# Strassen's seven products for a second group of tokens, and weight sums taken from the fp16 weights, in a fused attention and feed-forward kernel

## The chip, the cores and the metric

The kernel runs on one core of a Trainium2 chip. The metric is the device time of one execution in microseconds (us). The five engines of the core each have a queue of their own and take their instructions in order: TensorE (PE, matrix products; PEld is its weight load), VectorE (DVE), ScalarE (ACT), GpSimd (POOL) and SyncE (SP, which here only issues DMAs). An instruction that has to wait holds up all that stands behind it on its engine.

## The reference, cut to what matters

```python
for b in range(nb):                       # blocks of 64 positions
    intra = einsum('bhic,bhjc->bhij', qb, kb) * Dmask
    intra = einsum('bhij,bhjd->bhid', intra, vb)
    inter = einsum('bhid,bhde->bhie', qb * lam_pow, kv_state)
    out[:, :, sl] = intra + inter
    kv_state = lam_block * kv_state + einsum('bhsd,bhse->bhde', kb * rev_pow, vb)
...
h = x @ w_in                              # x: 3072 x 512 tokens, w_in: 512 x 2048
g = 0.5 * h * (1.0 + tanh(c * (h + 0.044715 * h * h * h)))
return g @ w_out                          # w_out: 2048 x 512
```

A decayed linear attention (4 batches, 8 heads, 768 positions, 64 columns a head) is followed by a feed-forward layer. The change concerns the last product, `g @ w_out`, for some of the tokens.

## The kernel before, in words

**Attention.** The work is cut into 24 steps (4 batches, 3 blocks of 256 positions, 2 halves of the heads). For step s, `prep` (L202) makes the decayed fp16 operands: q on DVE (L225), k on ACT (L230), v on POOL (L215). Steps 0 to 8 transpose them on PE (`stage_t`, L246, copied out at L253 or L255), later ones with a DMA (L234). `R(n, s)` (L590) issues the scores of step n (L275), the products of n and s (L310, L324, L333), the copy of the step's output to `xT` (L352, ACT) and the causal mask (L284, DVE, `PT`), then the update of the running state: `t` on DVE (L369, L372) and `u` on POOL (L379). `U(n)` does the second update. There is one buffer for the scores `Sps`, and there are six banks of PSUM for all else.

**Feed-forward.** Seven groups of tokens, of 512, 256, 256, 512, 512, 512 and 512. `queue_group(g)` appends small pieces of a group's work to a list, `filler`, and `fill(n)` pops n of them between the parts of attention, so that PE has work while other engines make its operands. The order is thus written out by hand: what `fill` issues, on every engine, stands in the engines' queues at that place. A piece `mm1` (L403) makes two of sixteen rows of blocks of the hidden layer for a group of 256 tokens (8 matmuls, L407) and their gelu (ACT, L411) into `gT`.

The second product is done in one of two ways. `mm2` (L416) is the plain one: for a tile of 128 tokens, 16 matmuls 512 wide (L422), 4 to a piece, then a copy (ACT, L428) and a DMA out (L429). `product` (L458) is Strassen's scheme: `gT` and `w_out` are cut in 2 x 2 blocks and seven products are made, each a piece of 8 matmuls 256 wide (L476). They need sums of blocks of `gT` (`sum_g`, L452, DVE, fp16, five sums, in two batches of hidden rows where the group has 256 tokens) and of `w_out` (`sum_wout`, L119). Products 3 and 4 take plain `gT` and a sum of weights, 5 and 2 a sum of `gT` (`gs`) and plain weights, 1, 7 and 6 sums on both sides. After product 2, ACT copies bank B (`m`, L483, L484) and DVE makes two sums with bank A (L487, L488); after product 1 DVE adds bank C (L496), after 6 bank D (L508), and the output leaves (L511). `behind(k, ...)` (L560) puts a batch of `sum_g` behind piece k of the group, counted from 0: for 256 tokens behind piece 5 (hidden rows 0 to 3) and piece 8 (rows 4 to 7); piece 8 is the first product, 3.

Before the change, groups 0 and 1 take `mm2`, groups 2 to 6 `product`.

**Weights.** `w_out` arrives by DMA in four parts of fp32 (`wo`, order 0, 2, 1, 3) and is cast to fp16, `w_out16`, by POOL and ACT (L115, L117). `sum_wout(j, m, eng)` makes half of one of the five sums of weight blocks on DVE (L123) from the fp32 parts: half 0 from parts 0 and 2, half 1 from parts 1 and 3. The five sums of half 0 stand ahead of step 4 (L666), those of half 1 in steps 8, 9 and 10 (L710).

The lines around the change are L662 to L713. Step n below is the turn of the loop at L699 with that n (steps 4 to 7 are written out above it). Sums are named (half, product): (1, 4) is the sum for product 4, half 1.

Of the kernel before, what the change touches and what calls it, by code (L numbers as in the profile page):

```python
# [15 lines left out]
def kernel(  # L16
# [11 lines left out]
    pin = tc.keep_in_program_order  # L28
# [32 lines left out]
    def load_step(s):  # L61
# [3 lines left out]
        for nm, src in (("q", q), ("k", k), ("v", v)):  # L65
# [8 lines left out]
    w_out16 = w16p.tile([P, NF, DM], FP16)  # L74


    HF, HE = NF // 2, DM // 2
    w_sum16 = w16p.tile([P, 5, HF, HE], FP16)
    W_SUMS = {3: ((0, 1), ALU.subtract, (1, 1)), 4: ((1, 0), ALU.subtract, (0, 0)),
              1: ((0, 0), ALU.add, (1, 1)), 7: ((1, 0), ALU.add, (1, 1)),  # L80
              6: ((0, 0), ALU.add, (0, 1))}
    w_slot = {m: i for i, m in enumerate(W_SUMS)}
    wstage = {}
# [25 lines left out]
    def cast_wout(j, eng):  # L109
        t = wstage[("o", j)]  # L110
        for i in range(2):
            dst = w_out16[:, 4 * j + 2 * i : 4 * j + 2 * i + 2, :]
            src = t[:, 2 * i : 2 * i + 2, :]
            if eng[i] is nc.scalar:
                pin(nc.scalar.activation(out=dst, in_=src, func=AF.Copy))  # L115
            else:
                pin(nc.gpsimd.tensor_copy(out=dst, in_=src))  # L117

    def sum_wout(j, m, eng):  # L119

        (f0, e0), op, (f1, e1) = W_SUMS[m]
        a, b = wstage[("o", j + 2 * f0)], wstage[("o", j + 2 * f1)]
        pin(eng.tensor_tensor(w_sum16[:, w_slot[m], 4 * j : 4 * j + 4, :],  # L123
                              a[:, :, e0 * HE : e0 * HE + HE], b[:, :, e1 * HE : e1 * HE + HE], op))


    lam_in = const.tile([P, H], FP32)
# [74 lines left out]
    def prep(s):  # L202
        prep_qk(s)
        prep_v(s)
# [8 lines left out]
    def prep_v(s):  # L213
        tv = a16p.tile([P, 2, HH, D], FP16, tag="v16", name=f"v16_{s}")
        pin(nc.gpsimd.tensor_tensor(wide(tv[:]), ld32[s][2][:], decay(dv, s), ALU.mult))  # L215
        a16[s] = a16[s] + (tv,)
        if s >= 6:
            load_ahead(s + 3)

    def prep_qk(s):  # L220
        q32, k32, _ = ld32[s]
        tqk = a16p.tile([P, 2, 2, HH, D], FP16, tag="qk16", name=f"qk16_{s}")
        tq, tk = tqk[:, 0], tqk[:, 1]
        q_eng = nc.gpsimd if s == 3 else nc.vector
        pin(q_eng.tensor_tensor(wide(tq), q32[:], decay(dq, s), ALU.mult))  # L225
        if s == 0:
            inverse(halves[0])
            odd(halves[1])
            inverse(halves[1])
        pin(nc.scalar.activation(out=wide(tk), in_=k32[:], func=AF.Copy))  # L230
        a16[s] = (tq, tk)
        if s >= FIRST_DMA_T:
            o = qkp.tile([P, 2, 2, 2, P], FP16, tag="qkT", name=f"qkT_{s}")
            pin(nc.sync.dma_start_transpose(out=o[:].rearrange("p a j h t -> p (a j h) t"),  # L234
                                            in_=tqk[:].rearrange("p a j h d -> p (a j h d)")))
            qkT[s] = o

    def stage_t(s):
        if s >= FIRST_DMA_T:
            return  # L240
        tq, tk = a16[s][:2]
        Tps = ps_M.tile([P, 2, 2, 2, P], FP16, tag="M", name="Tps")
        for i, t in enumerate((tq, tk)):
            for hp in range(2):
                for j in range(2):
                    pin(nc.tensor.transpose(Tps[:, i, j, hp, :], t[:, j, 2 * hp : 2 * hp + 2, :],  # L246
                                            ident[:]))
        o = qkp.tile([P, 2, 2, 2, P], FP16, tag="qkT", name=f"qkT_{s}")
        if s in (2, 3):
            pin(nc.scalar.activation(out=o[:, 0], in_=Tps[:, 0], func=AF.Copy))  # L250
            pin(nc.vector.tensor_copy(out=o[:, 1], in_=Tps[:, 1]))
        elif s in (1, 5, 6):
            pin(nc.scalar.activation(out=o[:], in_=Tps[:], func=AF.Copy))  # L253
        else:
            pin(nc.vector.tensor_copy(out=o[:], in_=Tps[:]))  # L255
        qkT[s] = o
# [131 lines left out]
    filler = []  # L388

    def queue_group(g):  # L390
        N = len(groups[g]) * SB
        NTAU = N // P
# [10 lines left out]
        def mm1(fs):  # L403
            Hps = ps_M.tile([P, per, N], FP32, tag="M", name="Hps")
            for i, f in enumerate(fs):
                for c in range(NC):
                    pin(nc.tensor.matmul(by_block(Hps[:, i, :]), w_in16[:, c, f * P : (f + 1) * P],  # L407
                                         x(c), start=(c == 0), stop=(c == NC - 1)))
            f = fs[0]
            dst = gT[:, f, :, :] if per == 2 else gT[:, f % HF, f // HF : f // HF + 1, :]  # L410
            pin(nc.scalar.activation(out=dst, in_=Hps[:], func=AF.Gelu_apprx_tanh))  # L411
# [4 lines left out]
        def mm2(tau, part):  # L416

            if not O2.get(tau):
                O2[tau] = [ps_M.tile([P, DM], FP32, tag="M", name="O2ps"), 0]
            for f in range(4 * part, 4 * part + 4):  # L420
                n = O2[tau][1]
                pin(nc.tensor.matmul(O2[tau][0][:], gT[:, f % HF, f // HF, tau * P : (tau + 1) * P],  # L422
                                     w_out16[:, f, :], start=(n == 0), stop=(n == NF - 1)))
                O2[tau][1] += 1
            if O2[tau][1] < NF:
                return
            o32 = otp.tile([P, DM], FP32, tag="o32", name="o32")
            pin(nc.scalar.activation(out=o32[:], in_=O2.pop(tau)[0][:], func=AF.Copy))  # L428
            pin(nc.sync.dma_start(out=out[row0 + tau * P : row0 + tau * P + P, :], in_=o32[:]))  # L429
# [115 lines left out]
        for i in range(HF):  # L545
            for fs in ([[i, i + HF]] if per == 2 else [[i], [i + HF]]):
                filler.append(lambda fs=fs: mm1(fs))
        if g == 1:
            for tau in range(NTAU):
                for part in (0, 2, 1, 3):  # L550
                    filler.append(lambda tau=tau, part=part: mm2(tau, part))
            return
        ms = ((3, 4, 5, 2), (1, 7, 6))
        order = [(m, p) for p in range(HN // P) for m in ms[0] + ms[1]]
        if g == len(groups) - 1:
# [30 lines left out]
    def fill(n):  # L586
        for _ in range(min(n, len(filler))):
            filler.pop(0)()

    def R(n, s):  # L590
        if n is not None:
            scores(n)
        products(n, s)
        if n is not None:
            causal(n)
        if s is not None and s % 2 == 1:
            g, i = group_of[s // 2]
            if i == len(groups[g]) - 1 and g > 0:
                queue_group(g)
        if n is not None:  # L600
            update(n, 0)

    def U(n):
        update(n, 1)
# [40 lines left out]
    update(3, 0)  # L645
    causal(3)
    queue_group(0)
    fill(8)
    cast_win(0, 0, 256, 256, c23, on_act=True)
# [13 lines left out]
        cast_win(j)  # L663
    DVE, ACT, POOL = nc.vector, nc.scalar, nc.gpsimd
    cast_wout(0, (POOL, POOL))
    for m in W_SUMS:  # L666
        sum_wout(0, m, DVE)
    fill(8)
    cast_wout(2, (ACT, ACT))
    cast_wout(1, (POOL, ACT))  # L670
    cast_wout(3, (POOL, ACT))
    fill(9)
    prep(4)
    stage_t(4)
    prep(5)
    fill(2)
    R(4, None)
    stage_t(5)
# [4 lines left out]
    stage_t(6)  # L683
    U(5)
    prep(7)
    fill(2)
    R(6, 5)
    U(6)
# [1 line left out]
    prep(8)  # L690
    fill(1)
    stage_t(7)
    fill(2)
    R(7, 6)
    U(7)
# [3 lines left out]
    for n in range(8, NSTEP + 1):  # L699
        m = n if n < NSTEP else None  # L700
        if m is not None:
            stage_t(n)
        if n + 2 < NSTEP:
            prep(n + 2)
        fill(2 if n <= 12 else 4)
        R(m, n - 1)
        fill(1)
        if m is not None:
            U(m)
        for p in {8: (3, 4), 9: (1, 7), 10: (6,)}.get(n, ()):  # L710
            sum_wout(1, p, DVE)
        fill(2 if n == 11 or n > 12 and n % 2 else 3)
    fill(len(filler))  # L713

# [28 lines left out]
```

## Time and profile before

| what | value |
|---|---|
| median of 6 executions | 205.3 us (204.9 to 205.92) |
| the profiled execution, its own time | 205.3 us |
| its span in the profile | 203.5 us |
| PE / DVE / ACT / POOL busy | 195.6 / 144.8 / 108.2 / 69.9 us |
| share of PE in the chain that ended last | 89% |
| L422, matmul 512 wide | 96 instructions, 21.9 us |
| L123, sum of weights | 10 instructions, 6 in 7.9 us and 4 in 6.0 us |
| L452, sum of `gT`, 128x512 | 50 instructions, 21.6 us |

The span runs from the first to the last instruction on the core; the execution's own time has 1.8 us more around it. Times in views are counted from the start of the span. In a timeline a row gives start, duration, engine, line, operation, output and inputs, shapes, count, and in brackets how long the engine had been idle and what ended that. Rows of one kind that follow each other are merged, so a row of "x2" has the time from the first's start to the last's end. A row's duration includes time in which the instruction has been issued and cannot go on. In the chain of waits a row gives start, length, engine, tile, line and number of instructions.

### The profile page before, as it was taken

The numbers are of one execution on the slowest core, as the hardware profiler recorded it, in microseconds if no ns is written. First come the engines' busy times: TensorE is split into PE (matmuls) and PEld (weight loads), VectorE is DVE, ScalarE is ACT, GpSimd is POOL, SyncE is SP. The second block draws the span as 40 slices with busy tenths as digits, with TensorE's granted clock in tenths as the row PEclk, the third lists the DMA queues.
The fourth block names the chain that finished last, engine by engine and source line by source line (L and its number), as shares of the span: only waits on it lengthen the run. The fifth ranks groups of instructions, "written<-read, shape, count | busy, mean of one in ns | idle before, by whom it ended". The sixth has DMA issues, their size and how long they took to land.

```text
span 203.5 us, 5595 instructions
## 1 busy us (share of the span) xinstructions
PE 195.6 (96%) x2325; PEld 127.6 (63%) x2325; DVE 144.8 (71%) x275; ACT 108.2 (53%) x204; POOL 69.9 (34%) x80
## 2 busy tenths in 40 slices
PE   7788999999999999999999999999999999999993
PEld 2456544456875788644688654788554788545882
DVE  4896726877699998929997828996739773236652
ACT  3365778475873573477722387641576431666210
POOL 4595123656586851336134404314412101000000
PEclk9999999999999999999999999999999999999999
DMA  5999999999999999997659993648340003300014
GB/s 151 297 324 389 385 386 377 284 291 311 333 257 231 291 247 147 233 277 184 64 155 228 236 264 95 147 114 134 87 97 0 3 0 103 108 0 0 3 47 159
DMA packets 63937, 37.85 MB, mean 186 GB/s; under 512 B 17576, under 2 KB 59048, under 8 KB 63912
## 3 DMA queue, kind: packets, MB, share of 16 engines
q1 hardware_dynamic: 63616, 37.23, 71.7%
q8 instruction: 18, 0.29, 0.6%
q10 hardware_dynamic: 296, 0.26, 0.4%
q14 instruction: 7, 0.06, 0.1%
HBM read 27.26 MB, written 6.29 MB: 165 GB/s over the span
## 4 chain that ended last, share of the span: by engine, by line
PE 89%; SPq 4%; DMA 4%; issue 1%; DVE 1%; ACT 1%
PE Hps L407 37%; PE O2ps L422 10%; PE MB L476 8%; PE MA L476 7%; PE MD L476 7%; SPq L68 4%; PE MC L476 4%; DMA wi<-in_moe_w_in_dram 4%; PE Sps L275 3%; PE Hps L522 3%; PE OK L333 3%; PE OK L324 3%; PE Tps L246 1%; PE OK L310 1%; PE ME L476 0%
## 5 line engine op out<-in xcount | busy, mean ns | idle before, releaser
L407 PE MATMUL Hps<-xT,w_in 128*128 128x512 f16 (+1 forms) x416 | 79.1, 346 | 0.0
L411 ACT ACTIVATE gT<-Hps 128x512 f16<-128x512 f32 x88 | 52.4, 597 | 22.6 <-PE Hps L407 21.8
L407 PEld LDWEIGHTS <-w_in 128*128 128x128 f16 x416 | 40.3, 98 | 33.5
L379 POOL TENSOR_TENSOR u<-t,lumask 128x256 f16<-128x256 f32 x40 | 31.3, 788 | 80.0 <-DVE t L372 53.4
L452 DVE TENSOR_TENSOR gs<-gT 128x512 f16<-128x512 f16 (+1 forms) x70 | 36.6, 587 | 10.8 <-ACT gT L411 10.6
L284 DVE TENSOR_TENSOR PT<-Sps,mask 128x1024 f16<-128x1024 f32 x24 | 29.2, 1217 | 16.9 <-PE Sps L275 16.8
L476 PEld LDWEIGHTS <-gs 128*128 128x128 f16 x360 | 34.9, 98 | 4.0
L215 POOL TENSOR_TENSOR v<-v,dv 128x512 f16<-128x512 f32 x24 | 29.2, 1218 | 4.2 <-DMA v<-in_v_dram 3.8
L352 ACT ACTIVATE xT<-OK 128x256 f16<-128x256 f32 x47 | 18.1, 453 | 18.9 <-PE OK L333 15.3
L422 PE MATMUL O2ps<-w_out,gT 128*128 128x512 f16 x96 | 21.9, 379 | 0.0
L230 ACT ACTIVATE qk<-k 128x512 f16<-128x512 f32 x24 | 15.0, 624 | 8.0 <-DMA k<-in_k_dram 8.0
L225 DVE TENSOR_TENSOR qk<-q,dq 128x512 f16<-128x512 f32 x23 | 19.2, 835 | 0.0
L483 ACT ACTIVATE m<-MB 128x512 f32<-128x512 f32 x9 | 5.4, 597 | 25.4 <-PE MB L476 25.4
L476 PE MATMUL MA<-w_sum,gT 128*128 128x256 f16 x144 | 17.5, 273 | 0.1
L476 PE MATMUL MD<-w_sum,gs 128*128 128x256 f16 x136 | 17.5, 273 | 0.0
L476 PE MATMUL MB<-w_out,gs 128*128 128x256 f16 x144 | 17.2, 273 | 0.0
L476 PEld LDWEIGHTS <-gT 128*128 128x128 f16 x144 | 14.0, 98 | 2.8 <-ACT gT L411 0.3
L422 PEld LDWEIGHTS <-gT 128*128 128x128 f16 x96 | 9.2, 98 | 9.9
L487 DVE TENSOR_TENSOR o<-MA,m 128x512 f32<-128x512 f32 x9 | 6.2, 689 | 12.7 <-ACT m L483 12.7
L372 DVE SCALAR_TENSOR_TENSOR t<-t,lamu,OK 128x64 f32<-128x64 f32 x64 | 14.6, 273 | 0.7
L275 PEld LDWEIGHTS <-qkT 64*64 64x64 f16 x384 | 6.1, 106 | 8.5 <-issue 4.9
L123 DVE TENSOR_TENSOR w_sum<-wo,wo 128x1024 f16<-128x1024 f32 x6 | 7.9, 1362 | 4.2 <-DMA wo<-in_moe_w_out_dram 4.2
(59 smaller groups left out, 167.4 us busy)
## 6 DMA issues: line engine op xcount, KB each, us to landing
q<-in_q_dram SPq DMA_DIRECT2D x24, 256.0 KB, 4.9
k<-in_k_dram SPq DMA_DIRECT2D x24, 256.0 KB, 4.8
v<-in_v_dram SPq DMA_DIRECT2D x24, 256.0 KB, 4.8
out_dram<-o SPq DMA_DIRECT2D x22, 256.0 KB, 4.4
wo<-in_moe_w_out_dram SPq DMA_DIRECT2D x4, 1024.0 KB, 9.5
wi<-in_moe_w_in_dram SPq DMA_DIRECT2D x4, 512.0 KB, 8.1
wi<-in_moe_w_in_dram SPq DMA_DIRECT2D x2, 1024.0 KB, 13.7
out_dram<-o SPq DMA_DIRECT2D x2, 128.0 KB, 1.9
```

Source lines behind the costliest of these rows:

```text
L215: pin(nc.gpsimd.tensor_tensor(wide(tv[:]), ld32[s][2][:], decay(dv, s), ALU.mult))
L225: pin(q_eng.tensor_tensor(wide(tq), q32[:], decay(dq, s), ALU.mult))
L230: pin(nc.scalar.activation(out=wide(tk), in_=k32[:], func=AF.Copy))
L284: pin(nc.vector.tensor_tensor(t[:].rearrange("p a b c d -> p (a b) (c d)"), Ss.pop(n)[:].rearrange("p a b c d -> p (a b) (c d)"), mask[:]. ...
L352: pin(nc.scalar.activation(out=d, in_=o, func=AF.Copy))
L372: pin(nc.vector.scalar_tensor_tensor(t[:, hp, :], state[half][:, hp, :], lamu[:, 2 * half + hp : 2 * half + hp + 1], K[:, hp, :], ALU.mult ...
L379: pin(nc.gpsimd.tensor_tensor(u[:], state[half][:].unsqueeze(2).to_broadcast([P, 2, 2, D]), lumask[:, 2 * half : 2 * half + 2, :].unsqueez ...
L407: pin(nc.tensor.matmul(by_block(Hps[:, i, :]), w_in16[:, c, f * P : (f + 1) * P], x(c), start=(c == 0), stop=(c == NC - 1)))
L411: pin(nc.scalar.activation(out=dst, in_=Hps[:], func=AF.Gelu_apprx_tanh))
L422: pin(nc.tensor.matmul(O2[tau][0][:], gT[:, f % HF, f // HF, tau * P : (tau + 1) * P], w_out16[:, f, :], start=(n == 0), stop=(n == NF - 1)))
L452: pin(nc.vector.tensor_tensor(gsum[m][:, i, :], block(T0, F0, i), block(T1, F1, i), op))
L476: pin(nc.tensor.matmul(dst, lhsT, rhs, start=(i == 0), stop=(i == HF - 1), skip_group_check=True))
```

## The change

Group 1 goes through `product` as groups 2 to 6 do: seven pieces in place of eight, with its ten sums of `gT` (batches behind its pieces 5 and 8), two ACT copies and four DVE sums from PSUM. One piece fewer is popped at the end of step 8.

`sum_wout` reads `w_out16` in place of the fp32 parts. The five sums of half 0 and (1, 6) stand after the casts, ahead of step 4; (1, 3) stands behind `prep(5)`, (1, 4) behind `prep(7)`, (1, 1) and (1, 7) behind `stage_t(7)`; those of steps 8 to 10 are gone.

```diff
     def sum_wout(j, m, eng):
 
         (f0, e0), op, (f1, e1) = W_SUMS[m]
-        a, b = wstage[("o", j + 2 * f0)], wstage[("o", j + 2 * f1)]
-        pin(eng.tensor_tensor(w_sum16[:, w_slot[m], 4 * j : 4 * j + 4, :],
-                              a[:, :, e0 * HE : e0 * HE + HE], b[:, :, e1 * HE : e1 * HE + HE], op))
+
+        def rows(f, e):
+            f = f * HF + 4 * j
+            return w_out16[:, f : f + 4, e * HE : e * HE + HE]
+
+        pin(eng.tensor_tensor(w_sum16[:, w_slot[m], 4 * j : 4 * j + 4, :], rows(f0, e0), rows(f1, e1), op))
@@
-        if g == 1:
-            for tau in range(NTAU):
-                for part in (0, 2, 1, 3):
-                    filler.append(lambda tau=tau, part=part: mm2(tau, part))
-            return
         ms = ((3, 4, 5, 2), (1, 7, 6))
@@
     cast_wout(0, (POOL, POOL))
-    for m in W_SUMS:
-        sum_wout(0, m, DVE)
     fill(8)
     cast_wout(2, (ACT, ACT))
     cast_wout(1, (POOL, ACT))
     cast_wout(3, (POOL, ACT))
+    for m in (6, 3, 4, 1, 7):
+        sum_wout(0, m, DVE)
+    sum_wout(1, 6, DVE)
     fill(9)
     prep(4)
     stage_t(4)
     prep(5)
+    sum_wout(1, 3, DVE)
     fill(2)
@@
     prep(7)
+    sum_wout(1, 4, DVE)
     fill(2)
@@
     stage_t(7)
+    sum_wout(1, 1, DVE)
+    sum_wout(1, 7, DVE)
     fill(2)
     R(7, 6)
@@
             U(m)
-        for p in {8: (3, 4), 9: (1, 7), 10: (6,)}.get(n, ()):
-            sum_wout(1, p, DVE)
-        fill(2 if n == 11 or n > 12 and n % 2 else 3)
+        fill(2 if n in (8, 11) or n > 12 and n % 2 else 3)
     fill(len(filler))
```

## The prediction

> **What bounds the kernel now.** I read the page's busy times, then the chain of waits, then the timelines of DVE, POOL and ACT around steps 6 to 9.
>
> ```profile
> PE 195.6 (96%) x2325; PEld 127.6 (63%) x2325; DVE 144.8 (71%) x275; ACT 108.2 (53%) x204; POOL 69.9 (34%) x80
> ```
>
> From 17.5 us to 199 the chain runs over PE but for some 2 us; here it is around group 1's second product:
>
> ```profile
> 58.28 0.35 PE Sps L275 x16
> ...
> 59.20 0.87 PE Hps L407 x8
> 60.07 4.32 PE O2ps L422 x20
> 64.39 0.35 PE Sps L275 x16
> ...
> 65.42 2.59 PE O2ps L422 x12
> 68.00 2.62 PE Hps L407 x24
> ...
> 79.02 1.75 PE MB L476 x16
> ```
>
> One piece follows the next without a gap: PE's work is the bound, and each wait that PE newly gets is added to the time. L422 takes 4.32 / 20 = 0.216 us an instruction, L476 1.75 / 16 = 0.109. DVE beside it:
>
> ```profile
> 57.18 1.39 DVE L225 TENSOR_TENSOR qk<-q,dq 128x512 f16<-128x512 f32 x1
> 58.68 1.23 DVE L284 TENSOR_TENSOR PT<-Sps,mask 128x1024 f16<-128x1024 f32 x1
> 59.83 0.88 DVE L372 SCALAR_TENSOR_TENSOR t<-t,lamu,OK 128x64 f32<-128x64 f32 x4
> 60.62 1.44 DVE L123 TENSOR_TENSOR w_sum<-wo,wo 128x1024 f16<-128x1024 f32 x1
> ```
>
> In step 8 DVE is never idle: q of step 10, mask of step 8, its four state updates, two sums of weights. POOL runs beside it:
>
> ```profile
> 57.99 1.49 POOL L215 TENSOR_TENSOR v<-v,dv 128x512 f16<-128x512 f32 x1
> 60.37 0.61 POOL L379 TENSOR_TENSOR u<-t,lumask 128x256 f16<-128x256 f32 x1 [0.90 <-DVE t L372]
> 60.94 1.59 POOL L379 TENSOR_TENSOR u<-t,lumask 128x256 f16<-128x256 f32 x1
> ```
>
> The same `u` takes 0.61 us and then 1.59, the second while DVE's sum of weights runs (60.62 to 62.06): it ends at 62.53, 0.47 after the sum. How group 2's first batch of `gs` fares, first on DVE:
>
> ```profile
> 73.93 0.83 DVE L452 TENSOR_TENSOR gs<-gT 128x512 f16<-128x512 f16 x1
> 73.93 2.01 DVE L452 TENSOR_TENSOR gs<-gT 128x512 f16<-128x512 f16 x2
> 77.47 1.75 DVE L452 TENSOR_TENSOR gs<-gT 128x512 f16<-128x512 f16 x5
> ```
>
> ```profile
> 73.01 1.46 POOL L379 TENSOR_TENSOR u<-t,lumask 128x256 f16<-128x256 f32 x1 [2.21 <-DVE t L372]
> 74.44 1.22 POOL L215 TENSOR_TENSOR v<-v,dv 128x512 f16<-128x512 f32 x1
> ```
>
> POOL's `u` ends at 74.47 and the first `gs` at 74.76, its `v` at 75.66 and the second `gs` at 75.94. So they take turns: a `gs` ends 0.28 after the POOL instruction ahead of it. Alone, five take 1.75: 0.42 for the first and 0.335 for each more.
>
> **What the Trainium skill says.** SBUF — State Buffer, section Who interferes with whom: "A DVE instruction with two SBUF inputs contends with a GpSimd instruction that reads SBUF", and the one that comes second blocks until the first is done. The rows above agree. Sums of weights, sums of `gT` and q are of that kind; the mask, `t`, the copies from PSUM and the additions of L487 to L508 have at most one SBUF input. VectorE: DVE Perf Modes, section The perf-mode tier table: `tensor_tensor` runs at twice the rate on 16-bit operands in SBUF, at the single rate on fp32. The trace agrees: an fp32 sum of weights alone took 1.21 us, a `gs` of the same 128x1024 in fp16 0.68, two of them 1.28, so 0.60 for each that follows.
>
> **The products.** Removed: 2 tiles x 16 x 0.216 = 6.91 us of PE. Added: 7 x 8 x 0.109 = 6.12. All on the path: -0.79. ACT loses two copies of 0.59 and gets 0.98 in two (L483, L484); its idle time covers this. SP issues two DMAs of the output as before, later; the loads stay in their steps. The fp32 parts' buffers come free with the casts, so that group 1's `gs` find theirs.
>
> **Sums of weights ahead of step 4.** Before, five fp32 sums end at 38.68 and q of step 4 takes 38.60 to 40.12, held by POOL's cast to 39.58. Afterwards (0, 6) waits for POOL's first casts, done at 31.35, in an idle time of 4.19 us. (0, 3) waits for ACT's two casts, which begin at 33.03 and take 1.05 each, overlapping: 35.03. POOL's cast at 34.76, with DVE idle, runs 1.03 and ends at 35.79; then four sums, 0.55 + 3 x 0.60, to 38.15; POOL's last cast, ready at 37.66, runs then, to 39.1; (1, 6) to 39.65; q of step 4 to 40.25. Behind this wait stand q and the transposes of step 4, which PE begins at 40.27. Cost: 0 to 0.7 us (if one more turn is lost), I take 0.1.
>
> **Sums in steps 4 to 7.** (1, 3) and (1, 4) lie in idle times of 0.80 and 0.99 us ahead of the masks of steps 4 and 6: nothing. Without that cover each would cost the mask 0.6, and PE needs it, or its freed `Sps`, over 1 us later. (1, 1) and (1, 7) are issued at 52.33, while POOL has `v` to 53.01, and end at 54.15; the mask of step 7 started at 53.83. DVE is 0.25 late from here. The transposed q and k of step 8, copied by DVE to 57.26 before and 57.5 now, are needed at 58.28: no stall.
>
> **The wait that comes.** The first batch of `gs` is issued behind q of step 10 and so ahead of the mask of step 8; the second behind the four `t`. Neither place held a `gs` before. With the 0.25, q of step 10 ends at 58.82. POOL's `v` has waited and takes its turn, 0.9, to 59.72. First batch: 0.28 + 4 x 0.335 = 1.62, to 61.34. Mask: from 61.27 to 62.49. `t` from 62.41; the first `u` starts 0.54 after that (60.37 - 59.83) and ends at 63.56; `gs` of product 5, second half, 63.85.
>
> PE: product 3 from 60.07 to 60.94 (its last weights need the gelu that ACT ends at 60.71, in time), product 4 to 61.82, half of product 5 to 62.26. Its fifth matmul needs the `gs` just computed: about 63.9 with 0.05 for the semaphore. PE stands for 1.64 us. Product 2's second half needs the next `gs`, 0.47 + 0.28 later, 64.6; PE gets there at 64.8. Step 9's scores start at 65.2, 64.39 before.
>
> Later waits. The third `gs` comes after a `v` of 0.9 and is there at 65.8, wanted at 66.7. L488 frees bank A at 68.3, for a piece of group 2 at 69.7; L508 frees bank D at 71.4, wanted at 72.6; the state of step 9 is ready at 70.5, wanted at 72.2. In step 10 the sum of weights (1.2) is gone, so group 2's `gs` start at 73.5, where they started at 73.93. No second stall. The sums gone from steps 8 to 10 give back DVE time that PE didn't wait for.
>
> **Sum.** -0.79 + 1.64 + 0.1 = +0.95 on a span of 203.5, so 204.4. The profiled execution took 205.3 with 1.8 around its span, the same as the median: 206.2.
>
> **The bounds of the unknown costs.** The wait for `gs` isn't in the trace of before. Lower end: no turn lost to POOL and no delay of 0.25; then q ends at 58.57, the first batch at 60.25, the mask at 61.4, the `gs` at 62.55, and PE waits 0.35. It can't be below nothing, since PE has no gap that it would fill. Upper end: one more POOL turn of 0.9 ahead of it, 2.5. I take 1.64, since each turn is taken from a row in which it occurs.
>
> **Rivals.**
> Forecast: PE waits 1.3 to 2.1 in product 5: 205.9 to 206.7. Chance 0.60.
> Rival 1, the turns don't fall as in the rows: DVE loses little to POOL and PE waits 0.3 to 1.2: 204.9 to 205.7. For: turns depend on tenths of a microsecond. Against: at 58.57 POOL's `v` has been waiting. 0.20.
> Rival 2, the other side: the `gs` is there when PE comes, and the matmuls count alone: 205.3 - 0.79 = 204.5. It decides once the second batch's first `gs` ends before 62.26. For: fp16 sums free DVE 10 x 0.6 us. Against: that time is freed in steps 8 to 10, mostly behind the place; in front of it 1.6 us of `gs` are added. 0.10.
> Rival 3: DVE's lateness grows, and the banks freed by L488 and L508 or the state of step 9 stop PE again by 0.5 to 1: 206.8 to 207.4. Margins are 1.2 to 1.7. 0.10.
>
> **How the numbers follow.** About 0.3% (0.6 us) is what a measurement of this kernel can tell from no change. Slower, over 205.9: 0.53 of the forecast's 0.60 and rival 3: 0.63. Within: 0.07 of the forecast and 0.19 of rival 1: 0.26. Faster: rival 2 and the rest of rival 1: 0.11. The range 204.8 to 206.9 leaves out rival 2 and most of rival 3, some 0.17.
>
> **What would show it.** In the profile after: MA to MD of group 1 with 56 matmuls near 60 to 68; in PE's timeline a hole of 1.3 to 2.1 us in product 5, ended by DVE's `gs`; a first batch of `gs` that starts near 59.7, behind POOL's `v`; step 9's scores near 65.2; no other new hole over 0.2. The forecast is wrong if that hole is under 0.8, or if PE stands elsewhere.

## The result, and the profile after

The changed kernel takes 206.4 us (median of 15 executions, 206.03 to 207.54), the kernel before 205.18 in the executions taken beside it (34, 204.68 to 206.2). The ratio is 1.0061, with a 95% interval of 1.0046 to 1.0077: slower by 1.2 us (0.9 to 1.6). Forecast was 206.2, slower.

The first two fences are from the page of the kernel after: busy times, then three of its rows, which count the whole kernel (bank B of groups 1 to 6, the plain product that only group 0 has left, the sums of weights).

```profile
PE 194.6 (95%) x2349; PEld 129.6 (63%) x2349; DVE 145.4 (71%) x289; ACT 107.8 (53%) x204; POOL 65.4 (32%) x80
```

```profile
L479 PE MATMUL MB<-w_out,gs 128*128 128x256 f16 x160 | 19.3, 273 | 1.5 <-DVE gs L455 1.5
...
L425 PE MATMUL O2ps<-w_out,gT 128*128 128x512 f16 x64 | 14.6, 379 | 0.0
L127 DVE TENSOR_TENSOR w_sum<-w_out 128x1024 f16<-128x1024 f16 x10 | 8.2, 864 | 6.0 <-POOL w_out L117 3.5
```

PE is busy 1.0 us less in a span that is 1.1 us longer, so the time is lost in a wait, and the page names one: 1.5 us of PE ahead of bank B, ended by DVE's `gs`. (Line numbers of the kernel after are 3 higher in this part: L479 was L476, L455 L452, L287 L284, L375 L372, L382 L379, L218 L215, L410 L407; L127 was L123. In the experiments they differ from these by up to 2.) The chain of waits after, at the same place as the one shown of before:

```profile
57.35 1.42 DVE qk L228
58.77 0.73 DVE gs L455
59.50 0.38 issue
59.88 1.42 DVE gs L455 x4
61.29 1.14 DVE PT L287
62.43 0.28 DVE t L375 x2
...
63.14 0.65 DVE gs L455
63.79 0.05 issue
63.84 1.48 PE MB L479 x12
65.32 0.35 PE Sps L278 x16
```

From step 7 to 63.8 us the chain runs over DVE, where it ran over PE before: q of step 10, the first batch of `gs`, mask, state, and the first `gs` of the second batch, with 0.05 to PE. Step 9's scores start at 65.32; before at 64.39. PE's timeline of the kernel after:

```profile
58.99 1.04 PE L410 MATMUL Hps<-xT,w_in 128*128 128x256 f16 x8
59.86 2.01 PE L479 MATMUL MA<-w_sum,gT 128*128 128x256 f16 x16
61.71 0.60 PE L479 MATMUL MB<-w_out,gs 128*128 128x256 f16 x4
63.84 1.48 PE L479 MATMUL MB<-w_out,gs 128*128 128x256 f16 x12 [1.53 <-DVE gs L455]
65.25 0.42 PE L278 MATMUL Sps<-qkT 64*64 64x128 f16 x16
```

Four matmuls of product 5 on the first batch's rows, then the hole, then the other four and product 2 in one go. DVE's first batch, then POOL beside it:

```profile
58.69 2.60 DVE L455 TENSOR_TENSOR gs<-gT 128x512 f16<-128x512 f16 x5
```

```profile
58.56 1.10 POOL L218 TENSOR_TENSOR v<-v,dv 128x512 f16<-128x512 f32 x1 [0.35 <-DMA v<-in_v_dram]
62.89 1.36 POOL L382 TENSOR_TENSOR u<-t,lumask 128x256 f16<-128x256 f32 x2 [3.22 <-DVE t L375]
64.22 1.22 POOL L218 TENSOR_TENSOR v<-v,dv 128x512 f16<-128x512 f32 x1
```

The first `gs`, issued at 58.69, ends behind the `v` that POOL has until 59.66.

**A measure that is steadier than the time.** The profiled executions differ by up to 1.5 us in when PE's work gets going (the scores of step 3 start at 16.05 us in e1 and at 17.52 in e6), and the times of one kernel gather in two groups about 1 us apart, called early and late here (of 43 executions of the kernel before, 31 lie at 204.74 to 205.75, median 205.17, and 12 at 205.96 to 206.79, median 206.2). So I also compare stages: the time from the start of the scores of step 8 to those of step 9, and on to step 10, as PE's timelines give them.

| kernel | 8 to 9 | 9 to 10 | both, against before | ratio of times (95%) |
|---|---|---|---|---|
| before | 6.10 | 6.24 | | |
| after | 7.08 | 6.27 | +1.01 | 1.0061 (1.0046 to 1.0077) |
| e1, sums of weights alone | 6.11 | 6.24 | 0.00 | 0.9999 (0.9983 to 1.0015) |
| e2, sums from fp32 | 8.59 | 7.06 | +3.31 | 1.0152 (1.0116 to 1.0188) |
| e3, no wait for `gs` | 5.38 | 7.18 | +0.22 | 1.0008 (0.9991 to 1.0025) |
| e4, `gs` behind the mask | 5.38 | 6.37 | -0.59 | 0.9976 (0.9961 to 0.9992) |
| e5, `v` later | 6.30 | 6.27 | +0.22 | 1.0016 (0.9994 to 1.0037) |
| e6, one more sum | 7.80 | 6.27 | +1.73 | 1.0128 (1.0094 to 1.0163) |
| e7, e4 with a `v` later | 5.38 | 6.27 | -0.69 | 0.9986 (0.9963 to 1.0009) |
| e8, products alone | 5.38 | 6.27 | -0.69 | 0.9981 (0.9964 to 0.9999) |

From the scores of step 4 to those of step 8 every kernel takes the same 15.76 us but for e2 (16.53) and e6 (15.97), and from step 10 to the last matmul every kernel takes 129.53, so what is won or lost in these stages goes into the time. Between the last matmul and the end of the span lie 3.41 us before, 3.40 in e1 and 3.55 to 3.59 in all kernels in which group 1 takes Strassen's products. These 0.15 us lie in the instructions with which the program ends, behind the last DMA issue; why is not settled. With them, 1.01 + 0.16 - 0.04 (an earlier start) comes to the 1.1 by which the span grew.

### The profile page after: what moved, and what is told of

Read it like the earlier page. It is cut to its first block, busy times and chain, and to the rows that moved or that the text cites. A ratio compares the mean times of both kernels' runs of the same rounds, so it can differ in the third digit from the quotient of the medians.

```text
span 204.6 us, 5657 instructions
## 1 busy us (share of the span) xinstructions
PE 194.6 (95%) x2349; PEld 129.6 (63%) x2349; DVE 145.4 (71%) x289; ACT 107.8 (53%) x204; POOL 65.4 (32%) x80
## 4 chain that ended last, share of the span: by engine, by line
PE 72%; DMA 12%; DVE 7%; SPq 6%; issue 1%; ACT 1%; DVEq 0%
PE Hps L410 30%; PE MB L479 8%; PE MD L479 8%; PE MA L479 7%; DMA wi<-in_moe_w_in_dram 7%; DMA q<-in_q_dram 5%; PE MC L479 4%; SPq L68 4%; PE Sps L278 3%; PE O2ps L425 3%; PE OK L336 3%; PE OK L327 2%; DVE qk L228 2%; DVE gs L455 1%; SPq L91 1%; DVE PT L287 1%
## 5 line engine op out<-in xcount | busy, mean ns | idle before, releaser
L410 PE MATMUL Hps<-xT,w_in 128*128 128x512 f16 (+1 forms) x416 | 79.1, 346 | 0.0
L410 PEld LDWEIGHTS <-w_in 128*128 128x128 f16 x416 | 40.2, 98 | 33.3
L382 POOL TENSOR_TENSOR u<-t,lumask 128x256 f16<-128x256 f32 x40 | 28.7, 724 | 83.9 <-DVE t L375 61.7
L455 DVE TENSOR_TENSOR gs<-gT 128x512 f16<-128x512 f16 (+1 forms) x80 | 42.1, 590 | 11.7 <-ACT gT L414 11.5
L479 PEld LDWEIGHTS <-gs 128*128 128x128 f16 x400 | 38.6, 98 | 6.2 <-DVE gs L455 1.8
L287 DVE TENSOR_TENSOR PT<-Sps,mask 128x1024 f16<-128x1024 f32 x24 | 29.2, 1217 | 13.8 <-PE Sps L278 13.8
L218 POOL TENSOR_TENSOR v<-v,dv 128x512 f16<-128x512 f32 x24 | 28.0, 1166 | 4.7 <-DMA v<-in_v_dram 3.0
L479 PE MATMUL MB<-w_out,gs 128*128 128x256 f16 x160 | 19.3, 273 | 1.5 <-DVE gs L455 1.5
L479 PE MATMUL MA<-w_sum,gT 128*128 128x256 f16 x160 | 19.5, 273 | 0.1
L479 PE MATMUL MD<-w_sum,gs 128*128 128x256 f16 x152 | 19.4, 273 | 0.0
L479 PEld LDWEIGHTS <-gT 128*128 128x128 f16 x160 | 15.5, 98 | 3.1 <-ACT gT L414 0.5
L375 DVE SCALAR_TENSOR_TENSOR t<-t,lamu,OK 128x64 f32<-128x64 f32 x64 | 14.7, 274 | 0.6
L425 PE MATMUL O2ps<-w_out,gT 128*128 128x512 f16 x64 | 14.6, 379 | 0.0
L127 DVE TENSOR_TENSOR w_sum<-w_out 128x1024 f16<-128x1024 f16 x10 | 8.2, 864 | 6.0 <-POOL w_out L117 3.5
L278 PE MATMUL Sps<-qkT 64*64 64x128 f16 x384 | 10.0, 222 | 0.7 <-DVE qkT L254 0.5
```

The lines of the kernel that those rows point to most:

```text
L278: pin(nc.tensor.matmul(Sps[half64(c), hl, hp, jk, :], o[half64(hl), 1, jk, hp, half64(c)], o[half64(hl), 0, :, hp, half64(c)], start=True, ...
L287: pin(nc.vector.tensor_tensor(t[:].rearrange("p a b c d -> p (a b) (c d)"), Ss.pop(n)[:].rearrange("p a b c d -> p (a b) (c d)"), mask[:]. ...
L382: pin(nc.gpsimd.tensor_tensor(u[:], state[half][:].unsqueeze(2).to_broadcast([P, 2, 2, D]), lumask[:, 2 * half : 2 * half + 2, :].unsqueez ...
L455: pin(nc.vector.tensor_tensor(gsum[m][:, i, :], block(T0, F0, i), block(T1, F1, i), op))
L479: pin(nc.tensor.matmul(dst, lhsT, rhs, start=(i == 0), stop=(i == HF - 1), skip_group_check=True))
```

## The experiments

My theory: the change gains some 0.8 us of matmuls and loses more in PE's wait for the first `gs` of the second batch, and this wait is as long as DVE is late, by its own new work ahead of it and by turns lost to POOL. Rivals: (A) the moved sums of weights make the loss; (B) place and turns fix the wait, and what lies further ahead is absorbed; (C) the products gain nothing, or DVE stops PE at the next place by as much.

### e1: the sums of weights alone

```diff
+        if g == 1:
+            for tau in range(NTAU):
+                for part in (0, 2, 1, 3):
+                    filler.append(lambda tau=tau, part=part: mm2(tau, part))
+            return
         ms = ((3, 4, 5, 2), (1, 7, 6))
@@
-        fill(2 if n in (8, 11) or n > 12 and n % 2 else 3)
+        fill(2 if n == 11 or n > 12 and n % 2 else 3)
```

> Only the second half of the change: sums of weights from fp16 at their new places, group 1 keeps mm2. Theory (the cost is PE's wait in product 5 for the second batch of gs, and the moved sums alone are hidden): the same as before within 0.2 us, 205.2 +- 0.2, DVE about 0.2 us late at the mask of step 7. Rival A (the moved sums and their waits for the casts make the loss themselves): 206 or more.

Measured: 0.9999 (0.9983 to 1.0015), and the stages as before to 0.01 us. Theory holds, rival A falls. Fp16 sums at new places are worth nothing by themselves here: DVE isn't the bound where they were, nor where they went. Its time is freed all the same: in step 8, where it was never idle before, it now stands idle for 3.22 us ahead of the mask of step 9 (DVE's timeline of e1), and nothing comes of that.

### e2: DVE later ahead of the `gs`

```diff
         def rows(f, e):
-            f = f * HF + 4 * j
-            return w_out16[:, f : f + 4, e * HE : e * HE + HE]
+            return wstage[("o", j + 2 * f)][:, :, e * HE : e * HE + HE]
```

> The changed kernel, but its sums of weights read the fp32 parts again, at the new places. Theory (DVE's lateness ahead of the gs goes into PE's wait one to one): the two sums of step 7 take 1.15 instead of 0.6 each, so DVE comes about 1.1 us later to the gs, PE's hole in product 5 grows by 0.8 to 1.2, and q of step 4 may be 0.4 late: 207.2 to 208. Rival B (the place of the gs and POOL's turns fix the wait, what lies further ahead is absorbed by idle time): 206.4 +- 0.3.

Measured: 1.0152 (1.0116 to 1.0188), 208.89 against 205.61 in the executions beside it, or 208.3 on the 205.2 that the expectation counts from: above what either expected. The hole ends later, as the theory has it, and PE runs slowly behind it (PE's timeline of e2, then stretches of it with sum rows left out; the column after the five busy times is PE's granted clock):

```profile
65.31 2.23 PE L478 MATMUL MB<-w_out,gs 128*128 128x256 f16 x12 [2.29 <-DVE gs L454]
```

```profile
62.40:65.30 2.90, 0.62 (x6) 0.31 (x4) 2.90 (x9) 0.00 (x0) 0.94 (x2) 1.00 0.98 224
65.30:66.00 0.70, 0.69 (x6) 0.63 (x7) 0.70 (x2) 0.00 (x0) 0.70 (x2) 0.92 1.12 265
66.00:67.00 1.00, 1.00 (x7) 0.69 (x5) 1.00 (x2) 0.00 (x0) 0.91 (x1) 0.50 1.12 284
67.00:68.00 1.00, 1.00 (x27) 0.59 (x29) 1.00 (x4) 0.42 (x1) 0.00 (x0) 0.50 1.02 275
68.00:69.00 1.00, 1.00 (x42) 0.83 (x33) 1.00 (x3) 0.45 (x2) 0.00 (x0) 0.50 0.64 178
69.00:70.00 1.00, 1.00 (x11) 0.87 (x10) 1.00 (x3) 0.77 (x2) 0.00 (x0) 0.85 0.18 37
```

From 65.9 to 69.3 the clock is 0.5: twelve matmuls take 2.23 where they take 1.48 in the kernel after. So of the 2.3 us by which the two stages exceed those of the kernel after, 0.8 are the longer hole (2.29 for 1.53) and the remaining 1.5 the clock; PE also waits 0.70 ahead of the scores of step 8, for the copy of their transposed operands, which stands behind the sums on DVE. The hole's 0.8 speaks for the theory against rival B, but the clock is a cost that neither had.

This cost doesn't come with every execution. The profiled one (209.43) has a mean granted clock of 0.992 over its span, which is what 3.4 us at half clock make of 207.6; one other (209.60) has 0.989; the remaining three, of 207.47, 208.88 and 208.89, have 1.0. The profiled one less 1.5 would be 207.9 (an estimate from these stages), and that and 207.47 lie in the theory's range. The 1.4 us between the three without a fall may be the two groups of times named above; no trace of them was kept.

The Trainium skill has such a cost (TensorE: Matmul & The Clock Gate, section What's actually happening): a gate sets PE's clock by how busy PE has been of late, passes half of the pulses after at least one idle window, and the full clock again after a busy one; the window is some 3.4 us long and runs freely. The granted 0.50 and the length of the dip agree. The idle time doesn't: the hole of e2 was 2.29 us, short of a window. A fall in some executions of one kernel and not in others would fit a window that runs freely, but no run here shows the window itself.

### e3: no matmul of group 1 waits for `gs`

```diff
-                lhsT = block(*G_PLAIN[m], i)[:, t] if m in G_PLAIN else gsum[m][:, i, t]
+                lhsT = (block(*G_PLAIN.get(m, (0, 0)), i)[:, t] if m in G_PLAIN or g == 1
+                        else gsum[m][:, i, t])
```

> The changed kernel with the products 5, 2, 1, 7 and 6 of group 1 on plain gT in place of the sums of gT, which DVE still makes (so these products, and group 1's output, are other values). No matmul waits for gs in group 1. Theory: the hole in product 5 is gone and what is left is the matmuls' gain, less a wait of up to 0.5 at step 10, where DVE frees bank C and makes the state: 204.4 to 204.9. Rival C (seven products are no cheaper than two plain tiles here, or DVE's load stops PE at the next place by as much): 205.5 to 206.4.

Measured: 1.0008 (0.9991 to 1.0025), or 205.4 on the expectation's 205.2: outside what the theory said, and just below rival C, whose range the interval reaches. Steps 8 to 9 take 5.38, so the hole in product 5 is gone and the matmuls' gain is there (0.72). But 9 to 10 takes 7.18 in place of 6.27. PE's timeline of e3:

```profile
66.96 2.16 PE L410 MATMUL Hps<-xT,w_in 128*128 128x256 f16 x16
69.61 1.05 PE L410 MATMUL Hps<-xT,w_in 128*128 128x256 f16 x8 [0.48 <-DVE t L375]
70.59 0.42 PE L278 MATMUL Sps<-qkT 64*64 64x128 f16 x16
```

The third piece of group 2 takes over a bank of PSUM from step 9, and waits for DVE to have read it for the state (`t`, 69.10 to 69.56). With the wait at product 5 gone, PE meets the same lateness of DVE one step later and pays 0.9. This is the second half of rival C, and I had put it at 0.5 at most. In the changed kernel this second wait doesn't show because PE has already lost the time.

### e4: the `gs` behind the mask

```diff
-        if per == 2:
+        if g == 1:
+            behind(7, 0, 8, (5, 2))
+            behind(8, 0, 8, (1, 7, 6))
+        elif per == 2:
             behind(5, 0, 4)
```

(`behind` and `sum_g` get a list of the products whose sums they make.)

> The changed kernel with other places for group 1's gs: sums 5 and 2 whole behind piece 7, that is behind the mask of step 8 and its first state update, sums 1, 7 and 6 whole behind product 3. Same work. Theory: the first gs ends near 61.6 and product 5 begins at 61.8, so the hole shrinks to 0.3 or less; with up to 0.3 at step 10 the time is 204.4 to 205.0, below both kernels. Rival B (POOL's turns make the gs late wherever it stands) or C: 205.5 to 206.4.

Measured: 0.9976 (0.9961 to 0.9992), 0.5 us below the kernel before (0.2 to 0.8) and 1.7 below the changed one. DVE, POOL and PE in e4:

```profile
58.97 1.21 DVE L287 TENSOR_TENSOR PT<-Sps,mask 128x1024 f16<-128x1024 f32 x1
60.11 0.46 DVE L375 SCALAR_TENSOR_TENSOR t<-t,lamu,OK 128x64 f32<-128x64 f32 x2
60.98 1.43 DVE L457 TENSOR_TENSOR gs<-gT 128x1024 f16<-128x1024 f16 x2 [0.41 <-ACT gT L414]
```

```profile
57.46 2.49 POOL L218 TENSOR_TENSOR v<-v,dv 128x512 f16<-128x512 f32 x2
```

```profile
61.99 1.91 PE L481 MATMUL MB<-w_out,gs 128*128 128x256 f16 x16
```

The mask runs at once behind q of step 10, in its usual 1.21, while POOL has its `v` until 59.95: it has one input in SBUF and takes no turn. The two sums that product 5 and 2 need are made whole as soon as the last gelu is there, and end at 62.41. PE makes products 5 and 2 in one go from 61.99: no hole. This is the same work: its order on DVE decides. What is left against e7 (below) is 0.1 at the third piece of group 2.

### e5: two instructions of POOL later

```diff
-            prep(n + 2)
+            (prep_qk if n in (8, 9) else prep)(n + 2)
@@
             U(m)
+            if n in (8, 9):
+                prep_v(n + 2)
```

> The changed kernel with POOL's v of step 10 behind the updates of step 8 and its v of step 11 behind those of step 9 (their loads move along). DVE's order is the same. Theory (a POOL instruction that holds DVE up ahead of the first batch of gs goes into PE's wait one to one): the first batch takes 1.8 instead of 2.6, all that follows is 0.8 earlier, PE's hole is 0.8 to 1.0 instead of 1.8, and the time is 0.5 to 1.0 below the changed kernel, 0.2 to 0.7 above the one before. Rival (turns with POOL cost nothing by themselves, DVE's own work makes the lateness): as the changed kernel, 1.2 above the one before.

Measured: 1.0016 (0.9994 to 1.0037), 0.3 above the kernel before, in the theory's range; the interval lies below the changed kernel's. (This expectation and the next give the hole of the changed kernel as 1.8: that is the wait of PE's weight load; PE's own was 1.53.) DVE, then PE, of e5:

```profile
58.45 1.75 DVE L455 TENSOR_TENSOR gs<-gT 128x512 f16<-128x512 f16 x5
60.13 1.21 DVE L287 TENSOR_TENSOR PT<-Sps,mask 128x1024 f16<-128x1024 f32 x1
```

```profile
62.81 1.48 PE L479 MATMUL MB<-w_out,gs 128*128 128x256 f16 x12 [0.74 <-DVE gs L455]
```

Without POOL's `v` the first batch takes 1.75 where it took 2.60, and PE's wait in product 5 is 0.74 where it was 1.53: the one turn goes into the time, one to one (stages 8 to 10: -0.78). The other `v` that was moved stands behind that place, and stage 9 to 10 is 6.27 as in the changed kernel. Rival B falls in its sharper form, that turns cost nothing.

### e6: one sum more

```diff
     sum_wout(1, 7, DVE)
+    sum_wout(1, 7, DVE)
     fill(2)
     R(7, 6)
```

> The changed kernel with the sum (1, 7) made twice in step 7, so that DVE comes 0.6 later to the gs. Theory, DVE's lateness one to one: the hole grows from 1.8 to 2.4 and the time by 0.6, to 1.8 above the one before. Rival (a hole past some 2 us also lowers PE's granted clock for some us, as the run with fp32 sums suggests, where it fell to 0.5 for 3 us after a hole of 2.3): 2.5 to 3.5 above the one before, with a dip of the clock near 65 us.

Measured: 1.0128 (1.0094 to 1.0163), 2.6 us, in the rival's range; but its profile shows no dip of the clock. PE's timeline of e6:

```profile
65.73 1.48 PE L479 MATMUL MB<-w_out,gs 128*128 128x256 f16 x12 [2.25 <-DVE gs L455]
```

In the stages the sum costs 0.72, near the 0.6 of the theory, and steps 4 to 8 take 0.2 more, since in this execution (1, 3) lost a turn to a `v`. With the closing 0.16 that makes 2.1 against the kernel before.

The rest of the 2.6 lies in which executions are compared. Five of the six lie within 208.27 to 208.47 and one at 207.32, and the profiled one, of 208.31, is one in which PE's work starts 1.3 late (scores of step 3 at 17.52, 16.25 in the kernel after); of the kernel before, most executions are in the early group. The early one less the median of the early group (205.17), and 208.31 less the median of the late group (206.2), are 2.1 to 2.2. That the other late ones are late starts too is not shown.

The rival is not out, though. Two of the six, of 208.32 and 208.47, have a mean granted clock of 0.992 and 0.989, as low as in the two executions of e2; their traces weren't kept. In the kernel before and in all other kernels no execution whose clock is on record lies below 0.996. So the length of the hole follows the theory, and a fall of the clock seems to come on top in some executions of e6 and not in others.

### e7: the `gs` behind the mask, and one `v` later

```diff
-            prep(n + 2)
+            (prep_qk if n == 9 else prep)(n + 2)
@@
             U(m)
+            if n == 9:
+                prep_v(n + 2)
```

(on e4)

> The kernel with the gs behind the mask, and POOL's v of step 11 behind the updates of step 9, so that it takes no turn between the sums 1, 7 and 6. Theory (what was left of the loss there is PE's wait of 0.2 for the state of step 9 on DVE): DVE is 0.9 earlier there, the wait goes, and the time is 0.2 to 0.4 below that kernel, 0.6 to 0.9 below the one before. Rival (the rest is something else): no change against that kernel, 0.5 below the one before.

Measured: stages -0.69 against before, the last wait is gone (6.27 for 9 to 10), and steps 8 to 10 take 0.1 less than in e4, not 0.2 to 0.4. The time is 0.9986 (0.9963 to 1.0009), 0.3 below the kernel before and not 0.6 to 0.9: it doesn't tell e7 from e4, nor from the kernel before.

### e8: the products alone

```diff
+        if g == 1:
+            return
         if per == 2:
             behind(5, 0, 4)
```

(on e3)

> The kernel without a wait for gs, and without group 1's ten sums of gT on DVE as well (the products take plain gT, so group 1's output is other values). Theory: only the matmuls' difference is left, 0.8 below the one before, since DVE is then 4 us less busy ahead of step 10. Rival C (seven products are no cheaper than two plain tiles here): 0 to 0.3 below.

Measured: stages -0.69, the time 0.9981 (0.9964 to 0.9999), 0.4 below with an interval of 0.0 to 0.7. By the time alone rival C would not be out; by the stages it is, and the 0.15 behind the last matmul takes part of the gain back. The products do gain, a little less than the 0.8 expected: product 3's last weights wait 0.1 for the gelu. That e7, with all sums on DVE, has the same stages shows that the sums can be hidden wholly.

## Why the prediction was right, point by point

- **PE is the bound, and each new wait of PE is added.** Right. In all kernels 129.53 us lie between step 10 and the last matmul, and the time moves with the stages.
- **The products, -0.79.** -0.69 (e8). The prediction had the gelu in time for product 3; PE waits 0.1 for it.
- **Sums ahead of step 4, 0.1.** The turns fell otherwise than forecast: the six sums ended at 38.64 (39.65), and q of step 4, which then lost a turn to POOL's last cast, ran from 38.74 to 40.08 (40.25). PE waited 0.23 for it, a new hole just over the 0.2 that the prediction allowed, but the start of PE's work differs by more between executions; e1 bounds the cost: 0 within 0.3. That the end came out near the forecast is in part luck.
- **Sums in steps 4 to 7, DVE 0.25 late.** The mask of step 7 started at 54.03, 53.83 before, with the rest of PE's work 0.05 earlier: 0.25. PE took 15.76 from step 4 to step 8, as before: nothing.
- **The wait that comes.** First batch to 61.29 (forecast 61.34), `gs` of product 5 at 63.79 (63.85), PE on at 63.84 (63.9). The hole, as the difference of the stages 8 to 9 of the changed kernel and e8, is 1.70 (1.64); the timeline's 1.53 leaves out that the four matmuls ahead of it have a row of 0.60, where four in a stream take 4 x 0.109. POOL's `v` began later than forecast, held by its load, and ended at 59.66 (59.72). It was issued at 58.56, only 0.13 ahead of the first `gs`, where the forecast had it waiting already: that it still went first is in part luck. e5 shows that its turn was in the hole, e4 that the place of the batches was.
- **Later waits, no second stall.** Right for the changed kernel (6.27 against 6.24). The margins were PE's own loss: e3 takes the first wait away and 0.9 appears at the third piece of group 2, through the state of step 9. The prediction counted the banks freed by L488 and L508 and the state of step 9, each with time to spare, but not this bank; rival 3 had named the state.
- **Sum.** +0.95 forecast; in the profile +1.1: 1.70 for 1.64, -0.69 for -0.79, and 0.16 behind the last matmul that was not in the sum, less the 0.1 ahead of step 4 that isn't seen. The mechanism was right; that the total is only 0.2 off owes something to errors of both signs.
- **Rivals.** 1 and 2 (DVE in time or nearly so) didn't occur: around step 8 every turn fell as in the rows of before. e4 is what rival 2 would have needed.
- **Upper end.** The bounds took a longer hole to cost its own length. e2 shows that a hole of 2.29 us, still below the upper end, can cost the clock as well, in some executions.

## What to carry to other kernels

Where PE has no gaps, an engine at its side that is busy all through a step is a second bound that the chain doesn't show: once its slack ahead of a point that PE will reach is used up, work added there costs its full length (e5, e6), and less work elsewhere on that engine gives nothing back (e1). To place it, go along that engine's queue from the last slack to the instruction that PE waits for, and count turns with GpSimd as length; then move what PE doesn't need yet behind what it needs (e4: the same work, 1.7 us less than in the changed kernel). Taking away one wait shows the next one only when it is tried (e3).

## What the runs showed of the hardware that I had not expected

In e2's profile, after PE had idled for 2.29 us, its granted clock fell to 0.5 for 3.4 us, beginning 0.6 us after it went on. Holes of 1.53 us (the changed kernel) and 2.25 us (e6) show no fall in their profiles. By the mean clock of each execution it is not the kernel alone that decides: two of the five executions of e2 and two of the six of e6 lie at 0.992 or 0.989, the others of both at 0.997 or more, and the changed kernel's fifteen at 0.996 or more. So a hole of some 2.3 us seems to cost the clock in some executions of one and the same kernel and not in others. A window that runs freely, as the section named under e2 has it, would make it a matter of where a hole falls; no run here shows where a window begins, so what decides is not settled.
